# An mLSTM block feeding a two-layer FFN: another order of the front, and low weight words made by ScalarE

## The chip, the cores and the metric

The kernel runs on one core of a Trainium2 chip. The metric is the device time of one execution in microseconds (us), the median of several runs. Engines are named as in the profile: PE is TensorE's matmul part and PEld its weight load, DVE is VectorE, ACT is ScalarE, POOL is GpSimd, SP is SyncE, which issues nearly all DMAs.

## The reference

An mLSTM recurrence over 4 batches, 8 heads, 768 steps and a head size of 40 gives `y`; its 3072 rows of 320 numbers go through a feed-forward network of width 2048 with a piecewise square as activation:

```python
for t in range(S):
    m_new = np.maximum(f_gate[:, :, t] + m, i_gate[:, :, t])
    f_stab = np.exp(f_gate[:, :, t] + m - m_new)
    i_stab = np.exp(i_gate[:, :, t] - m_new)
    C = f_stab * C + i_stab * np.einsum('bhd,bhe->bhde', vt, kt)
    n = f_stab * n + i_stab * kt
    y[:, :, t] = o * np.einsum('bhde,bhe->bhd', C, qt) / np.maximum(np.abs(nq), 1.0)
...
h = x @ w_in
g = np.where(h >= 1, h, np.where(h <= -1, 0.0, (h + 1) ** 2 / 4))
return g @ w_out
```

The attention inputs are float32. The two weight matrices are float64; the kernel loads their words as they are and makes float32 numbers of them itself.

## The kernel before, in words

**Units.** The sequence is cut into 6 chunks of 128 steps. A unit `n` is one chunk of one batch: `n = 4 * chunk + batch`, 24 in all. A unit gives 128 rows of `x`; four units of one chunk make a block of 512 rows, `X[j]`, in a high part `xh` and a rest `xl`.

**FFN.** For each block `j` and each of 16 slices `fc` of the width, `mm1` (line 744) makes 8 matmuls into a PSUM tile `psh` (two of them exist), ScalarE makes `Relu` and square of it and VectorE the result `r`, which also frees the `psh` tile. `mm2` (line 765) runs two slices behind (`LAG`) and adds the product of `r` and the second weights into four `pso` tiles. In block 0 the result `r` is used as it is (8 matmuls named `pso<-ow,r`); later it is split in two parts, `gh` and `gl`.

**Weight pieces.** The weights come in 16 pieces, in the order of `W_ORDER`: in 0, in 1, out 0, in 2, out 1, in 3 and so on. Here piece k is the k-th of that order. "in i" holds what slices 2i and 2i+1 need in `mm1`, "out i" the same for `mm2`. `load_w` issues the DMA of a piece (768 KB or 640 KB) into `wraw`, which has two buffers. `convert` makes float32 of it: in `words` (line 372) ScalarE makes `mg` (an `Abs`), VectorE takes the sign half by a bitwise AND, GpSimd makes the low half (`halves[:, :, 0]`), VectorE limits `mg` and joins everything with a shift and an OR (`SCALAR_TENSOR_TENSOR win<-mg,win` or `ow<-mg,ow`). For "in" pieces `split` (line 392) then makes the high part `wh` (ScalarE copy) and the rest `wl` (VectorE subtraction).

**The front.** Before the FFN starts, units 0 to 3 are worked through in an order that is written out by hand in `STEPS`. Each step's instructions stand on their engine's queue in that order (`InOrder`; such instructions have line 85 in the profile, the others line 82). The letters that matter: `E`, `A` make the exponents in PSUM and `x` their `Exp` on ScalarE (`Abc`, or `A` for unit 3); `s` the scores and `m` their product with the decays on VectorE; `u` the output matmuls, `y` the division on VectorE (from `z` to `y` in the profile), `z` the transposes and `t` the copies into `xh` and `xl`; `v` a scaling on GpSimd; `w` the number of dummy matmuls that `hot` puts ahead of the next group. `c` converts the words of piece 0, and asks for piece 2; `e` and `d` make its `wh` and `wl`. `b` is `batch_maxima`, the running maximum of the gates of chunks 1 to 4, which sends its result through four small DMAs to `m_b`; `g1` is `batch_sums` (line 199), six VectorE instructions and the store of `a_d`, from which the decays `Abc` of later units are loaded. `batch_tail` (line 211), seven VectorE instructions, and `batch_exps`, which makes the factors `G` and `nA` from transposes, run after the first `mm1`.

**What follows the front.** Loads for chunk 1 are issued; then the loop over slices begins. In block 0 each slice is preceded by `split_next` until `DUE(fc) = 3 + fc` pieces are converted, and each converted piece asks for the piece after the next. `behind(("x", "act"), ("x", "dve"))` puts these conversions on ScalarE and VectorE behind the last `xh`, `xl` copies of a unit that was traced before them. `slot` places the attention work of units 4 to 23 between the slices. The order on each engine outside the front is fixed when the program is built, by a planner with a timing of its own.

Of the kernel before, what the change touches and what calls it, by code (L numbers as in the profile page):

```python
# [23 lines left out]
P = 128  # L24
# [30 lines left out]


STEPS = (
# [3 lines left out]
)  # L61

HALF = 64
# [35 lines left out]
def mlstm_ffn_kernel(ctx, tc, qk, qn, vk, og, fi0, fi, fib, w_in, w_out, cst, out):  # L99
# [37 lines left out]
                            base=0, channel_multiplier=-1)  # L137
    half = const.tile([P, 1], F32, name="half")
    nc.vector.memset(half, 0.5)


    a_d = dr.tile([NC, NSEQ, L], F32, name="a_d")
# [109 lines left out]
    def run(steps):  # L252
        for _ in steps:
            pass
# [47 lines left out]
    def gate_tail(c):  # L302
        i, m, a, ac, al, ex = gtail.pop(c)
        dh = m[:, :L]
        eng = nc.vector
        eng.tensor_tensor(out=a, in0=i, in1=m[:, 1:], op=ALU.subtract)
        eng.tensor_tensor(out=a, in0=a, in1=al, op=ALU.subtract)
        nc.gpsimd.tensor_copy(ex[0:32], a)
        yield
        eng.tensor_tensor(out=dh, in0=ac[:, L - 1:].broadcast_to([NSEQ, L]), in1=ac, op=ALU.subtract)  # L310
        eng.tensor_tensor(out=dh, in0=dh, in1=a, op=ALU.add)
        yield
        eng.tensor_tensor(out=ex[32:64], in0=dh, in1=al[:, L - 1:].broadcast_to([NSEQ, L]), op=ALU.add)
        eng.tensor_tensor(out=dc[:, c:c + 1], in0=ac[:, L - 1:], in1=al[:, L - 1:], op=ALU.add)
# [57 lines left out]
    def words(out, raw):  # L372

        n = raw.shape[1] * raw.shape[2] // 2
        hi = raw.rearrange("p k (f w) -> p (k f) w", w=2)[:, :, 1]
        quarter = raw.rearrange("p k f -> p (k f)").bitcast(U16).rearrange("p (f w) -> p f w", w=4)
        out = out.rearrange("p k f -> p (k f)").bitcast(I32)
        halves = out.bitcast(U16).rearrange("p (f w) -> p f w", w=2)  # L380
        mg = stage.tile([P, n], F32, name="mg", bufs=1)
        nc.scalar.activation(mg, hi.bitcast(F32), AF.Abs, scale=65536.0)
        nc.vector.tensor_scalar(out=halves[:, :, 1], in0=quarter[:, :, 3], scalar1=0x8000, scalar2=None,
                                op0=ALU.bitwise_and)

        nc.gpsimd.tensor_scalar(out=halves[:, :, 0], in0=quarter[:, :, 1], scalar1=1 / 8192, scalar2=-4095.5 / 8192,
                                op0=ALU.mult, op1=ALU.add)
        nc.vector.tensor_scalar_max(mg, mg, TINY)
        nc.vector.scalar_tensor_tensor(out=out, in0=mg.bitcast(I32), scalar=3, in1=out,
                                       op0=ALU.logical_shift_left, op1=ALU.bitwise_or)  # L390

# [7 lines left out]
    def load_w(kind, i):  # L399
        if kind == "in":  # L400
            n = 2 * P
            raw = stage.tile([P, 3, 2 * n], I32, name="wraw", bufs=2)
            at = nc.sync.dma_start(raw.rearrange("p k f -> p (k f)"), w_in[i])
        else:
            raw = stage.tile([P, 2, 2 * DM], I32, name="wraw", bufs=2)
            at = nc.sync.dma_start(raw.rearrange("p k f -> p (k f)"), w_out[i])
        raws[kind, i] = raw
        return at

    def convert(kind, i):  # L410
        raw = raws.pop((kind, i))
        if kind == "in":
            sl = slice(2 * i * P, 2 * (i + 1) * P)
            w = stage.tile([P, 3, 2 * P], F32, name="win", bufs=1)
            words(w, raw)
            yield
            yield from split(wh[:, :, sl], wl[:, :, sl], w)
        else:
            of[i] = ow.tile([P, 656], F32, name="ow")[:, :2 * DM].rearrange("p (k e) -> p k e", k=2)
            words(of[i], raw)  # L420
            if 2 * i >= PLAIN_FC:
                yield
                yield from split_out(i)
# [101 lines left out]
    def load_A(n):  # L525
        if n >= NS:
            return
        c, b = divmod(n, B)
        t = T.setdefault(n, {})
        t["A"] = ld.tile([P, H, L], F32, name="Abc", bufs=3)  # L530
        src = a_d[c, b * H:(b + 1) * H]
        mark[n, "A"] = nc.sync.dma_start(t["A"], src.unsqueeze(0).broadcast_to([P, H, L]))
# [265 lines left out]

    InOrder.on = True
    mains = [None] * B  # L800

    for what in STEPS.split():
        n = int(what[1]) if what[1:2].isdigit() else 0
        hh = int(what[2:] or 0)
        if what == "Lg":
            first_gates()
        elif what == "Lf":
            load_batch()
        elif what == "Lc":
            nc.sync.dma_start(cs_t, cst[0:120, P:])  # L810
        elif what == "Li":
            nc.sync.dma_start(ident, cst[:, :P])
        elif what == "Lo":
            load_og(0)
        elif what[:2] == "Lq":
            load_qk(hh)
        elif what[:2] == "Lv":
            load_v2(hh)
        elif what[:2] == "Lw":
            mark["load"] = load_w(*W_ORDER[hh])  # L820
        elif what[0] == "s":
            score_mm(n)
        elif what[0] == "m":
            score_mul(n, hh)
        elif what[0] == "g":
            if n:
                batch_sums()
            else:
                run(gate_sums(n))
        elif what[0] == "b":  # L830
            batch_maxima()
        elif what[0] == "k":
            run(gate_tail(n))
        elif what[0] == "h":
            gate_exps(n)
        elif what[0] == "A":
            add_sums(n)
        elif what[0] == "E":
            exponents(n)
        elif what[0] == "p":  # L840
            first_sums()
        elif what[0] == "v":
            scale1(n)
        elif what[0] == "o":
            sigmoid(0)
        elif what[0] == "x":
            decay(n, hh)
        elif what[0] == "c":
            rest = convert(*W_ORDER[nw])
            next(rest)  # L850
            load_w(*W_ORDER[nw + 2])
            nw += 1
        elif what[0] in "ed":
            next(rest, None)
        elif what[0] == "w":
            heat = int(what[1:])
        elif what[0] in "uytz":
            if what[0] == "u":
                mains[n] = main(n)
            next(mains[n])  # L860
    InOrder.on = False
    with behind("load"):
        load_og(1)
        load_v(4)
        load_qk(4)
        load_qk(5)
        for n in range(4, 4 + NA):
            load_A(n)
    for i in range(FRONT - EARLY, FRONT):
        with behind(("x", "act"), ("x", "dve"), ("v", "pool")):  # L870
            slot(i)
# [7 lines left out]
    for x in range(NG + LAG):  # L879
        j, fc = divmod(x, NFC)  # L880
        if x < NG:
            if j == 0:
                while nw < min(len(W_ORDER), DUE(fc)):
                    split_next()
                if nw == len(W_ORDER) and late is None:
                    stages.close()
                    late = ctx.enter_context(tc.tile_pool(name="late", bufs=1, side="right"))
            if fc == 0:
                ops[j] = [ps_o.tile([P, 512], F32, name="pso") for _ in range(NTC)]
            if j == 1 and fc % 2 == 0 and fc < PLAIN_FC:  # L890
                with tc.issue_after(mark["r", "act"].ins), tc.issue_after(mark["r", "dve"].ins):
                    for _ in split_out(fc // 2):
                        pass
            if x == GATES_AT:
                load_gates(later, NC - 1, NC)
                steps = gate_steps(NC - 1)
            if x >= GATES_AT:
                with tc.issue_after(mark["r", "dve"].ins):
                    next(steps, None)
            r = mm1(j, fc)  # L900
            if x == 0:
                with tc.issue_after(mark["r", "dve"].ins):
                    batch_tail()
                    batch_exps()
            with behind(("v", "pool")):
                slot(FRONT + x)
            gs[x] = parts(r) if j or fc >= PLAIN_FC else (r,)
        if x >= LAG:
            j, fc = divmod(x - LAG, NFC)
            mm2(ops[j], fc, *gs.pop(x - LAG))  # L910
            if fc == NFC - 1:
                store(j, ops.pop(j))
# [58 lines left out]
```

## Time and profile before

| | us |
|---|---|
| median of 3 runs | 518.64 (517.13 to 519.9) |
| the profiled execution | 517.97 |
| its span, first to last instruction | 516.2 |
| mean granted TensorE clock | 0.979 |

The span is shown in three parts by the way the work lies: the front up to about 33.5 us, block 0 of the FFN with the conversions and units 4 to 7 up to about 143 us, and the other five blocks. "Idle before" in a row is the time in which the engine had nothing to do before that instruction, with the work that ended it. A row of the timeline gives start, duration, engine, line, operation, output and inputs.

### The profile page before, as it was taken

Reading aid. Unit: us, or ns where it says so; the run is one execution under the profiler, and the core shown is the slowest. Engines: PE = TensorE matmul, PEld = TensorE weight load, DVE = VectorE, ACT = ScalarE, POOL = GpSimd, SP = SyncE. Lnnn points to the kernel's source line nnn. Section 1 sums busy time; section 2 is a strip of 40 time slices with the busy share of each in tenths; the row PEclk is TensorE's granted clock in tenths of the full one; section 3 lists DMA queues with packets and bytes.
Section 4 is the critical chain, followed back from the end, with each engine's and each line's share of the span. In section 5 each row is a group of like instructions: output and inputs, shape, how many; then the busy total and the mean of one; then the engine's idle time right before and its main releaser. Section 6 shows DMA issues by size and latency. Waiting matters only on the chain.

```text
span 516.2 us, 8817 instructions
## 1 busy us (share of the span) xinstructions
PE 490.7 (95%) x3396; PEld 419.4 (81%) x3399; DVE 343.0 (66%) x621; ACT 289.1 (56%) x560; POOL 135.9 (26%) x136
## 2 busy tenths in 40 slices
PE   8985999889898999999999998999999999999996
PEld 3763877778677989988889988889888889988986
DVE  4789896679758776759696657756756745444332
ACT  4525884436087555676645567555377554455553
POOL 2324531343433333323142314403230210000000
PEclk8987999979999999999999999999999999999999
DMA  8868664364441303323223423113522000010001
GB/s 227 257 183 307 161 189 138 115 193 150 131 146 40 107 27 96 118 66 111 65 78 83 133 80 118 68 53 96 170 81 77 16 1 1 0 52 1 1 2 51
DMA packets 29646, 51.48 MB, mean 100 GB/s; under 512 B 10060, under 2 KB 19940, under 8 KB 29604
## 3 DMA queue, kind: packets, MB, share of 16 engines
q1 hardware_dynamic: 29604, 50.92, 32.4%
q8 instruction: 27, 0.44, 0.4%
q14 instruction: 15, 0.12, 0.1%
HBM read 46.80 MB, written 4.04 MB: 98 GB/s over the span
## 4 chain that ended last, share of the span: by engine, by line
PE 85%; DVE 6%; ACT 5%; DMA 3%; issue 1%; SPq 0%; ACTq 0%; DVEq 0%
PE pso L82 33%; PE psh L82 33%; PE psa L82 15%; ACT Abc L82 1%; PE pso L85 1%; DMA raw<-in_qk 1%; ACT L82 1%; PE psa L85 1%; DVE ow L82 1%; DMA wraw<-in_w_in 1%; PE psh L85 1%; ACT r L82 1%; DVE win L82 1%; DMA out<-r 1%; ACT sig L82 0%
## 5 line engine op out<-in xcount | busy, mean ns | idle before, releaser
L82 ACT ACTIVATE r<-psh,half 128x512 f32<-128x512 f32 x96 | 65.4, 685 | 111.7 <-PE psh L82 111.4
L82 DVE SCALAR_TENSOR_TENSOR r<-psh,r 128x512 f32<-128x512 f32 x96 | 65.8, 686 | 71.5 <-ACT r L82 71.3
L82 PE MATMUL psh<-xh,wh 128*128 128x512 f32 x288 | 104.3, 418 | 6.7 <-DVE r L82 6.1
L82 PE MATMUL pso<-oh,gh 128*128 128x320 f32 x320 | 100.6, 317 | 2.4 <-ACT gh L82 2.1
L82 PE MATMUL psh<-xh,wl 128*128 128x512 f32 x288 | 99.8, 401 | 0.0
L82 PE MATMUL pso<-ow,gh 128*128 128x320 f32 x320 | 99.2, 312 | 0.0
L82 PE MATMUL pso<-oh,gl 128*128 128x320 f32 x320 | 94.0, 311 | 1.6 <-DVE gl L82 1.6
L82 DVE TENSOR_TENSOR gl<-r,gh 128x512 fp32r<-128x512 f32 x80 | 62.2, 779 | 40.5 <-ACT gh L82 40.4
L82 ACT CAST gh<-r 128x512 fp32r<-128x512 f32 x80 | 49.4, 618 | 51.0 <-DVE r L82 50.4
L82 PEld LDWEIGHTS pso<-oh,gh 128*128 128x128 f32 x320 | 60.1, 188 | 7.4 <-ACT gh L82 2.5
L82 PEld LDWEIGHTS psh<-xh,wl 128*128 128x128 f32 x288 | 55.2, 192 | 13.1 <-DVE wl L85 0.4
L82 PEld LDWEIGHTS psh<-xh,wh 128*128 128x128 f32 x288 | 51.8, 194 | 15.2 <-DVE r L82 6.8
L82 PEld LDWEIGHTS pso<-ow,gh 128*128 128x128 f32 x320 | 60.2, 188 | 2.8
L82 PE MATMUL psh<-xl,wh 128*128 128x512 f32 x192 | 62.3, 405 | 0.0
L82 ACT ACTIVATE r<-r 128x512 f32<-128x512 f32 x96 | 60.4, 632 | 2.5
L82 PEld LDWEIGHTS pso<-oh,gl 128*128 128x128 f32 x320 | 58.9, 188 | 2.1 <-DVE gl L82 1.9
L82 ACT ACTIVATE Abc<-Abc,nA 128x128 f32<-128x128 f32 x160 | 49.9, 391 | 0.2
L82 POOL TENSOR_TENSOR v<-vk,G 128x328 f32<-128x328 f32 x36 | 30.6, 856 | 58.3 <-issue 45.9
L82 PEld LDWEIGHTS psh<-xl,wh 128*128 128x128 f32 x192 | 36.8, 192 | 8.6
L82 PE MATMUL pso<-ow,r 128*128 128x320 f32 x128 | 38.5, 443 | 0.5 <-DVE ow L82 0.5
L82 POOL TENSOR_SCALAR_AFFINE_SELECT Abc<-Abc 128x1024 f32<-128x1024 f32 x20 | 25.4, 1275 | 48.3 <-DMA Abc<-a_d 46.1
L82 POOL TENSOR_TENSOR m<-m 128x1024 bf16<-128x1024 f32 x12 | 24.4, 2037 | 46.4 <-DVE m L82 46.4
(203 smaller groups left out, 681.0 us busy)
## 6 DMA issues: line engine op xcount, KB each, us to landing
Abc<-a_d SPq DMA_DIRECT2D x20, 512.0 KB
raw<-in_qk SPq DMA_DIRECT2D x48, 160.0 KB
vk<-in_vk SPq DMA_DIRECT2D x20, 324.0 KB
wraw<-in_w_in SPq DMA_DIRECT2D x8, 768.0 KB
wraw<-in_w_out SPq DMA_DIRECT2D x8, 640.0 KB
sig<-in_og SPq DMA_DIRECT2D x6, 640.0 KB
out<-r SPq DMA_DIRECT2D x24, 160.0 KB
qn<-in_qn SPq DMA_DIRECT2D x20, 180.0 KB
```

What stands on the lines that cost most here:

```text
L82: r = getattr(self.engine, name)(*args, **kwargs)
L85: r = getattr(self.engine, name)(*args, **kwargs)
```

## The change

The low half of each weight piece is made by ScalarE (`Identity` with a scale and a bias tile `less`) instead of GpSimd. `words` becomes a generator that stops after the ScalarE part and, in the front, once more before the join. The order of the front is new: piece 0 (`c0`, five steps) and piece 1 (`c1`, five steps) are both converted in it, `b` comes earlier, `y`, `z`, `t` steps of units 0 to 2 stand elsewhere, and `batch_tail` becomes a front step, `k1`, behind `g1`. Piece 2 is asked for in the first `c` step, piece 3 after the loads for chunk 1.

```diff
 STEPS = (
     "Lg Li Lo Lq0 Lv0 Lq1 Lw0 Lf Lq2 Lv2 Lq3 Lw1 Lc o w9 E0 g0 p A0 k0 x00 w2 s0 x01 m00 w1 E1 A1 h0 v0 x10 m01 w2 s1 "
-    "x11 v1 m10 c w2 u0 m11 b w2 E2 A2 x20 w2 s2 y0 x21 v2 m20 m21 w2 u1 z0 w2 E3 A3 x30 e w2 s3 v3 y1 x31 t0 m30 m31 "
-    "w2 u2 z1 y2 w2 u3 t1 z2 y3 w2 t2 z3 t3 d g1 "
+    "Lg Li Lo Lq0 Lv0 Lq1 Lw0 Lf Lq2 Lv2 Lq3 Lw1 Lc o w9 E0 g0 p A0 k0 x00 w2 s0 x01 m00 w1 E1 A1 h0 v0 x10 m01 b w2 s1 "
+    "x11 v1 m10 w2 u0 m11 c0 w2 E2 A2 x20 y0 w2 s2 x21 v2 c0 c0 w2 u1 m20 m21 z0 w2 E3 A3 t0 x30 c0 y1 w2 s3 v3 x31 c1 z1 "
+    "c0 m30 m31 t1 w2 u2 c1 y2 c1 z2 w2 u3 t2 c1 y3 w2 z3 t3 c1 g1 k1 "
 )
...
+    less = const.tile([P, 1], F32, name="less")
+    nc.vector.memset(less, -4095.5 / 8192)
...
         nc.scalar.activation(mg, hi.bitcast(F32), AF.Abs, scale=65536.0)
+        nc.scalar.activation(halves[:, :, 0], quarter[:, :, 1], AF.Identity, bias=less, scale=1 / 8192)
+        yield
         nc.vector.tensor_scalar(out=halves[:, :, 1], in0=quarter[:, :, 3], scalar1=0x8000, scalar2=None,
                                 op0=ALU.bitwise_and)
-        nc.gpsimd.tensor_scalar(out=halves[:, :, 0], in0=quarter[:, :, 1], scalar1=1 / 8192, scalar2=-4095.5 / 8192,
-                                op0=ALU.mult, op1=ALU.add)
         nc.vector.tensor_scalar_max(mg, mg, TINY)
+        if front:
+            yield
...
-            words(w, raw)
+            yield from words(w, raw)
...
-            words(of[i], raw)
+            yield from words(of[i], raw)
...
         elif what[0] == "k":
-            run(gate_tail(n))
+            if n:
+                batch_tail()
+            else:
+                run(gate_tail(n))
...
         elif what[0] == "c":
-            rest = convert(*W_ORDER[nw])
-            next(rest)
-            load_w(*W_ORDER[nw + 2])
-            nw += 1
-        elif what[0] in "ed":
-            next(rest, None)
+            if n not in pieces:
+                pieces[n] = convert(*W_ORDER[n])
+            next(pieces[n], None)
+            if not nw:
+                load_w(*W_ORDER[2])
+                nw = 2
...
             load_A(n)
+        load_w(*W_ORDER[3])
...
                 with tc.issue_after(mark["r", "dve"].ins):
-                    batch_tail()
                     batch_exps()
```

More of the change, by code (lines that the diff above doesn't have):

```diff
@@ L800, in mlstm_ffn_kernel @@
     mains = [None] * B
+    pieces = {}
     for what in STEPS.split():
```

1 row of the table STEPS is left out of this document.

## The prediction, made before the changed kernel ran

> **What bounds the kernel now.** I read the page first: its chain of work that ended last says whose time the span is made of.
>
> ```profile
> PE 85%; DVE 6%; ACT 5%; DMA 3%; issue 1%; SPq 0%; ACTq 0%; DVEq 0%
> ```
>
> TensorE holds 85% of the chain, so a time is only to be had where it stands still or runs slowly. The windows show where that is among the stages that the change touches (the columns: window, its length, then busy time of PE, PEld, DVE, ACT and POOL, the granted clock, DMA share and GB/s).
>
> ```profile
> 39.00:45.20 6.20, 0.08 (x1) 0.00 (x0) 5.99 (x11) 4.45 (x7) 1.50 (x2) 0.88 0.73 262
> 45.20:52.00 6.80, 6.80 (x17) 5.03 (x18) 6.34 (x13) 3.15 (x6) 4.85 (x4) 0.61 1.01 354
> 52.00:64.00 12.00, 12.00 (x62) 9.66 (x61) 9.87 (x13) 9.99 (x26) 6.60 (x6) 1.00 0.68 160
> 64.00:76.00 12.00, 12.00 (x63) 8.97 (x61) 11.47 (x16) 10.44 (x19) 3.41 (x3) 1.00 0.69 205
> 97.00:112.00 15.00, 11.86 (x73) 9.76 (x72) 12.40 (x23) 6.04 (x13) 5.67 (x6) 0.77 0.65 206
> ```
>
> Two holes are to be seen: 39 to 45.2, where TensorE does nothing and VectorE is busy for 5.99 of 6.20 us, and 97 to 112, with 3.14 us idle. Both are followed or accompanied by a low clock (0.61 and 0.77). Between them TensorE has no idle time at all. The timeline of PE shows the first hole from both sides:
>
> ```profile
> 33.56 2.07 PE L82 MATMUL psh<-xh,wh 128*128 128x512 f32 x4 [0.57 <-ACT xh L85]
> ...
> 38.68 0.40 PE L82 MATMUL psh<-xh,wl 128*128 128x512 f32 x1
> 45.20 1.22 PE L82 MATMUL psh<-xh,wh 128*128 128x512 f32 x2 [6.12 <-DVE r L82]
> ```
>
> Slices 0 and 1 of `mm1` run from 33.56 to 39.08 (5.52 us); slice 2 needs a `psh` tile, and so the first `r` of VectorE. The chain of waits gives that `r` and the price of the cold clock after it:
>
> ```profile
> 44.46 0.70 DVE r L82
> ...
> 45.20 3.78 PE psh L82 x8
> 48.98 2.98 PE pso L82 x8
> 51.96 1.86 PE psh L82 x8
> ...
> 58.90 2.15 PE pso L82 x8
> ```
>
> The same eight matmuls take 3.78 us, then 1.86; the eight of `mm2` 2.98, then 2.15. The slow clock costs (3.78 - 1.86) + (2.98 - 2.15) = 2.75 us on top of the 6.12.
>
> What VectorE does before that `r` is in its timeline:
>
> ```profile
> 26.46 0.42 DVE L85 TENSOR_TENSOR xl<-psa,xh 128x256 fp32r<-128x256 f32 x1 [2.50 <-ACT xh L85]
> ...
> 34.30 0.96 DVE L85 TENSOR_TENSOR wl<-win,wh 128x768 fp32r<-128x768 f32 x1
> 35.18 0.28 DVE L85 TENSOR_TENSOR fi_b<-fi_b,m_b 128x128 f32<-128x128 f32 x1
> 35.38 0.53 DVE L82 TENSOR_SCALAR ow<-wraw 128x640 uint16<-128x640 uint16 x1
> ...
> 39.79 0.21 DVE L85 TENSOR_SCALAR ah_b<-fi_b 128x128 f32<-128x128 f32 x1
> 40.04 0.23 DVE L85 TENSOR_SCALAR ah_b<-ah_b 128x128 f32<-128x128 f32 x1
> 40.30 0.42 DVE L85 TENSOR_TENSOR_SCAN ac_b<-rst,ah_b 128x128 f32<-128x128 f32 x1
> ```
>
> The front's last copies end at 34.3. From there to 44.46, 10.2 us, VectorE works off `wl` of piece 0, `batch_sums`, pieces 2 and 1, and the first words of piece 3.
>
> **The change part by part.** *Piece 1 into the front.* Its three word instructions on VectorE and the `wl` of piece 0 are what the front gains; the views of the tiles `win` and `mg` give the durations (minimum, median, maximum in ns):
>
> ```profile
> L82 DVE TENSOR_SCALAR win<-wraw x7: 596/974/1470, 37.2 to 117.1; 128x768 uint16<-128x768 uint16 x7
> ```
>
> ```profile
> L82 DVE TENSOR_SCALAR mg<-mg x15: 441/490/1425, 35.8 to 133.4; 128x640 f32<-128x640 f32 x8, 128x768 f32<-128x768 f32 x7
> L82 DVE SCALAR_TENSOR_TENSOR ow<-mg,ow x8: 804/1266/1661, 42.8 to 134.3; 128x640 int32<-128x640 int32 x8
> L82 DVE SCALAR_TENSOR_TENSOR win<-mg,win x7: 942/1305/1577, 38.4 to 119.0; 128x768 int32<-128x768 int32 x7
> ```
>
> Ahead of the first `mm1` stand, newly, the AND (0.60), the limit (0.49) and the join (0.94) of piece 1 and the `wl` of piece 0 (0.96): 3.0 us. I take minima, since the low words leave GpSimd, and the long values lie where it works on the same piece. The idle 2.50 us before 26.46 could hide most of it, so 0 is the lower bound. Against that, the `Abs` and low words of piece 1 stand on ScalarE ahead of `t1`, and `z2` ahead of `u3` on TensorE, with `y2` behind two conversion steps; the upper bound is 4.5. I take 3.0: the first `mm1` starts at 36.6 and the copies of `t3` end at 37.3. Piece 0's own words only move; `b` fills the time before the second scores. `b` also sends its four small DMAs before piece 2's load and no longer behind it on SP's queue; I count nothing for that but that `batch_sums` won't wait for `m_b`. Piece 3 is asked for behind the loads of chunk 1 on that queue, among them one that waits until `sig` is free; I cost it at nothing, since its conversion isn't ahead of the first `r` any more.
>
> *From `t3` to the first `r`.* In VectorE's queue now stand `wl` of piece 1 (0.96), `g1` (two subtractions of 0.28, 0.21, 0.23, the scan with 0.42, and one more instruction of this shape at 0.28: 1.7), `k1` (one scan, 0.42, and six of at most 0.28: 2.1) and, since it is traced ahead of `mm1`, the words of piece 2 (0.53 + 0.44 + 0.80 = 1.8): 6.5 us, in place of 10.2. The first `r` runs from 43.8 to 44.5, and slice 2 starts at 44.5 in place of 45.20: **-0.7**. If the planner puts `r` ahead of piece 2 and the front grows by nothing, slice 2 starts at 45.20 - 0.7 - 1.8 - 3.0 = 39.7: -5.5. If the front grows by 4.5, +0.8. Slices 0 and 1 end at 36.6 + 5.5 = 42.1, so the hole is 2.4 us and not 6.12. Whether the clock holds over it is read from the second hole, where a wait of 1.77 was enough:
>
> ```profile
> 106.01 2.07 PE L82 MATMUL psa<-raw 40*128 40x128 f32 x14 [1.77 <-DVE hv L82]
> ```
>
> ```profile
> 108.08 5.69 PE psh L82 x16
> ```
>
> Sixteen matmuls took 5.69 us there, at 1.86 for eight they take 3.72. So the clock stays low after 2.4 us and I count **0** for it, with -2.75 as the other end. The Trainium skill (TensorE: Matmul & The Clock Gate, section "Why this matters for your kernels") would have the clock drop only after gaps of more than about 3 us; by that rule the shrunken hole would keep the clock and the sum would be 2.75 us lower. The row at 108.08, slow after 1.77 us, speaks against it, and I go by the row.
>
> *Low words on ScalarE, and what follows later.* `batch_tail` ends at 37.3 + 0.96 + 1.7 + 2.1 = 42.1, so the factors `G` and `nA` come earlier; ScalarE and GpSimd show what they hold up:
>
> ```profile
> 55.11 0.93 ACT L82 ACTIVATE mg<-wraw 128x768 f32<-128x768 f32 x1
> ...
> 56.92 4.79 ACT L82 ACTIVATE Abc<-Abc,nA 128x128 f32<-128x128 f32 x16
> ...
> 70.95 0.79 ACT L82 ACTIVATE mg<-wraw 128x640 f32<-128x640 f32 x1
> ```
>
> ```profile
> 48.06 3.94 POOL L82 TENSOR_SCALAR_AFFINE_SELECT Abc<-Abc 128x1024 f32<-128x1024 f32 x3 [1.66 <-DMA Abc<-a_d]
> ```
>
> The decays of units 4 and 5 ran at 56.92, though the first selected `Abc` was there at about 49.4. With the factors early they run at 49.4, 7.5 us sooner. At the second hole this matters: piece 11, which slice 12 needs, stands behind unit 4's last copies.
>
> ```profile
> 100.22 0.48 ACT L82 CAST xh<-psa 128x384 fp32r<-128x384 f32 x1
> ```
>
> ```profile
> 106.44 0.96 DVE L82 TENSOR_TENSOR wl<-win,wh 128x768 fp32r<-128x768 f32 x1
> ```
>
> From the copy at 100.22 to the end of `wl`, 107.40, are 7.2 us; a low word on ScalarE adds 0.9 to this, as it lies behind the `Abs` and not beside it. If the copy comes 7.5 us sooner, `wl` ends at about 100.8, and attention work fills most of the time from 97. The hole is worth 3.14 of idle time and 5.69 - 3.72 = 1.97 of clock, 5.1 in all; I take two thirds, **-3.4** (bounds 0 and -5.1).
>
> The low words themselves have no row on ScalarE. The nearest is `mg`, which reads the same words: 0.93 and 0.79. In the two windows from 52 to 76 ScalarE has 9.99 + 10.44 = 20.4 of 24.0 us; the four `mg` from 55.11 to 70.95 get four companions, 2 x 0.93 + 2 x 0.79 = 3.4, and 23.9 of 24 would be full. The earlier decays take about 3 of it away, into 45.2 to 52, where ScalarE has 6.80 - 3.15 = 3.65 idle. Cover is left, but thin: **+0.5**, bounds 0 and +5.4 (below). GpSimd loses sixteen instructions and gets nothing; what stands behind them in its queue (selections, scalings) can only come sooner, and no idle time of TensorE names GpSimd, so 0. That VectorE is disturbed less by GpSimd is worth nothing of its own while TensorE has no idle time.
>
> **The sum**: -0.7 + 0 - 3.4 + 0.5 = -3.6. The profiled execution took 517.97 us (span 516.2 and 1.8 around it), so 514.4; the median, 518.64, lies 0.7 above it. Forecast 514.4. A measurement of this kernel can tell about 0.5%, 2.6 us, from no change: faster is below 516.0, slower above 521.2.
>
> **The rivals.**
>
> - *Everything opens up (0.13).* `r` goes ahead of piece 2, the front grows by half (1.5), the clock holds and the second hole closes: -0.7 - 1.8 - 1.5 - 2.75 - 5.1 = -11.9, 506.1. For it: both holes come from VectorE's backlog. Against it: the 1.77 us row.
> - *The clock alone (0.09).* All as in the forecast, but the hole of 2.4 us is too short to lower the clock: 514.4 - 2.75 = 511.6. For it: the clock was low after 6.12 us at the first place, and at the second the 1.77 us came on top of other short waits (3.14 in all). Against it: the hole at the second place was no single long one and the clock fell all the same.
> - *The gain stays in the front (0.24).* The longer front eats the shorter queue, and the second hole stays since piece 11 still stands behind unit 4, whose place in the slices is unchanged: -0.7 + 0.9 + 0.5, 518.7. This is also the case in which the change does not do what it says: the planner may order the queues behind the front as before.
> - *ScalarE becomes the bound (0.16).* If the decays do not leave 52 to 76, ScalarE is full there and `r` comes late; it decides from the point at which the work in this stretch reaches its 24.0 us; then each of the four companions shows on TensorE: 3.4, and one wait long enough for the clock adds the 1.97 of the sixteen slow matmuls. Without the second hole's gain that is +5.4 - 0.7: 522.7. For it: 23.9 of 24. Against it: the free 3.65 us before 52. The Trainium skill (ScalarE: Activation LUTs, section "Rules for kernel authors") speaks for this rival: it puts additions and multiplications by constants on VectorE and not on ScalarE. No row of this case has such a step on ScalarE.
>
> **How the numbers follow.** The forecast, with its own range of 511 to 517, has 0.38; it gives 0.33 to faster and 0.05 to within 0.5%. The first and the second rival are faster (0.13 and 0.09), the third within (0.22, and 0.02 slower), the fourth slower (0.13, and 0.03 within). Faster 0.55, same 0.30, slower 0.15. The range leaves out the far half of the first rival and of the fourth, and the far ends of the single terms: 506 to 522.
>
> **What would show it.** A first `mm1` at 36 to 37 and its slice 2 before 45, with an idle time of 1 to 3 us ahead of it; `g1`, `k1` and piece 2 ahead of the first `r` on VectorE; `Abc` of unit 4 at about 49; PE idle by less than 1.5 us in the 15 us around slice 12. Wrong it would be if PE waits for ScalarE's `r` between 50 and 75, if the front ends after 38, or if the second hole is as wide as before.

## The result, and the profile after

The changed kernel takes 523.93 us (median of 4 runs, 523.76 to 528.05), the kernel before 519.27 in the same comparison: a ratio of 1.0126, with a 95% interval of 1.0091 to 1.0161. It is slower by 1.3%, where 514.4 had been forecast and "slower" had a chance of 0.15; the time lies above the range (506 to 522). The profiled execution took 523.76 us, 5.8 more than the one of before, with a span of 521.9 and a granted clock of 0.968. One execution of e8 (523.88 us, the profiled one) and one of e12 (534.64) ran at a low clock and took more than 1.5% longer than the fastest of their kernel; the medians, ratios and stages below leave them out.

The chain of work that ended last has the same shares as before within 2 points, so the loss is again to be looked for where TensorE stands still or runs slowly:

```profile
PE 83%; DVE 6%; ACT 6%; DMA 3%; issue 1%; SPq 1%; ACTq 0%; DVEq 0%
```

The windows of the changed kernel (window, length, busy time of PE, PEld, DVE, ACT, POOL, clock, DMA share, GB/s):

```profile
43.90:49.07 5.17, 2.27 (x9) 1.51 (x7) 4.31 (x11) 3.77 (x6) 1.57 (x2) 0.83 0.69 214
49.07:56.00 6.93, 6.93 (x16) 5.05 (x17) 6.00 (x12) 4.90 (x8) 3.41 (x3) 0.56 1.01 370
64.00:76.00 12.00, 12.00 (x61) 8.82 (x60) 6.55 (x11) 11.97 (x27) 0.00 (x0) 1.00 0.47 128
97.00:113.00 16.00, 13.41 (x81) 10.90 (x78) 11.12 (x21) 9.44 (x18) 2.28 (x3) 0.90 0.44 140
```

And the last of these windows in the kernel before:

```profile
97.00:113.00 16.00, 12.86 (x77) 10.59 (x76) 12.40 (x23) 6.62 (x14) 6.40 (x7) 0.79 0.61 197
```

Three things are to be seen. The hole ahead of slice 2 is shorter, and the clock behind it low all the same (0.56). The second hole is as it was, 2.59 us idle of 16 and 3.14 before. And ScalarE is busy for 11.97 of 12 us between 64 and 76, while TensorE is busy for all 12: TensorE does not wait for it.

The front is read from TensorE's timeline. First the kernel before, then the changed one; the first row of each is the start of `u0`, the front's first output product.

```profile
14.69 1.88 PE L85 MATMUL psh<-ow,Abc 128*128 128x41 f32 x16
28.06 1.95 PE L85 MATMUL psa<-ow,A 128*128 128x41 f32 x16
```

```profile
13.71 1.88 PE L85 MATMUL psh<-ow,Abc 128*128 128x41 f32 x16
25.74 0.52 PE L85 MATMUL pso<-ident,y 128*128 128x128 f32 x3 [1.62 <-DVE y L85]
31.65 0.88 PE L85 MATMUL psa<-ident,y 128*128 128x128 f32 x3 [2.91 <-DVE y L85]
33.17 3.48 PE L85 MATMUL psa<-ow,A 128*128 128x41 f32 x16
38.39 0.90 PE L85 MATMUL psh<-ident,y 128*128 128x128 f32 x3 [0.90 <-DVE y L85]
39.87 1.22 PE L82 MATMUL psh<-xh,wh 128*128 128x512 f32 x2 [0.57 <-ACT xh L85]
49.07 1.22 PE L82 MATMUL psh<-xh,wh 128*128 128x512 f32 x2 [2.90 <-DVE r L82]
52.65 3.59 PE L82 MATMUL pso<-ow,r 128*128 128x320 f32 x8
```

The same program run twice puts `u0` at 13.71 and at 12.46 (e12 below), so stages are best measured from `u0`. The first `mm1` came 33.56 - 14.69 = 18.87 us behind it before and 39.87 - 13.71 = 26.16 after: the front grew by 7.3 us. Product `u3` (`psa<-ow,A`) came 6.1 us later and took 3.48 us in place of 1.95. Ahead of it stands the transpose `z2`, which waits 2.91 us for `y2`. VectorE's timeline shows why `y2` is late:

```profile
15.22 1.27 DVE L85 TENSOR_TENSOR_SCAN m_r<-fi_r,m_r 32x512 f32<-32x512 f32 x1 [3.00 <-DMA fi_r<-in_fi]
...
28.78 0.60 DVE L85 TENSOR_SCALAR win<-wraw 128x768 uint16<-128x768 uint16 x1
29.27 0.55 DVE L85 TENSOR_SCALAR mg<-mg 128x768 f32<-128x768 f32 x1
...
31.01 0.49 DVE L85 TENSOR_TENSOR y<-pso,sz 128x320 f32<-128x320 f32 x1
31.42 0.95 DVE L85 SCALAR_TENSOR_TENSOR win<-mg,win 128x768 int32<-128x768 int32 x1
...
40.30 0.29 DVE L85 TENSOR_TENSOR xh<-psh,xh 64x128 fp32r<-64x128 f32 x1
...
47.12 0.53 DVE L82 TENSOR_SCALAR ow<-wraw 128x640 uint16<-128x640 uint16 x1 [0.72 <-DMA wraw<-in_w_out]
...
48.32 0.69 DVE L82 SCALAR_TENSOR_TENSOR r<-psh,r 128x512 f32<-128x512 f32 x1
```

`b` stands at the head of the queue for 3.00 us until `fi_r` has landed; piece 1's AND and limit (28.78 and 29.27) stand ahead of `y2`, which ends with the row at 31.01, and its join (31.42) ahead of `y3`. At the end, the first `r` has the AND of piece 4 and a limit ahead of it, and the AND waits for its transfer.

### The profile page after: what moved, and what is told of

It reads as the page before. It is cut to its first block, busy times and chain, and to the rows that moved or that the text cites. A ratio compares the mean times of both kernels' runs of the same rounds, so it can differ in the third digit from the quotient of the medians.

```text
span 521.9 us, 8808 instructions
## 1 busy us (share of the span) xinstructions
PE 493.9 (95%) x3396; PEld 423.1 (81%) x3399; DVE 335.1 (64%) x622; ACT 304.3 (58%) x576; POOL 113.6 (22%) x120
## 4 chain that ended last, share of the span: by engine, by line
PE 83%; DVE 6%; ACT 6%; DMA 3%; issue 1%; SPq 1%; ACTq 0%; DVEq 0%
PE psh L82 33%; PE pso L82 33%; PE psa L82 15%; DMA raw<-in_qk 2%; ACT L82 1%; PE psa L85 1%; ACT r L82 1%; ACT Abc L82 1%; DMA wraw<-in_w_out 1%; PE psh L85 1%; DVE gl L82 1%; ACT sig L82 1%; PE pso L85 1%; SPq L85 0%; DVE win L82 0%
## 5 line engine op out<-in xcount | busy, mean ns | idle before, releaser
L82 PE MATMUL pso<-oh,gl 128*128 128x320 f32 x320 | 95.3, 312 | 2.8 <-DVE gl L82 2.8
L82 DVE TENSOR_TENSOR gl<-r,gh 128x512 fp32r<-128x512 f32 x80 | 63.8, 799 | 40.6 <-ACT gh L82 40.4
L82 ACT CAST gh<-r 128x512 fp32r<-128x512 f32 x80 | 49.4, 617 | 52.3 <-DVE r L82 51.5
L82 POOL TENSOR_SCALAR_AFFINE_SELECT Abc<-Abc 128x1024 f32<-128x1024 f32 x20 | 23.9, 1199 | 58.9 <-DMA Abc<-a_d 53.6
```

What stands on the lines that cost most here:

```text
L82: r = getattr(self.engine, name)(*args, **kwargs)
```

## The experiments

All in three rounds against the kernel before, which had medians of 518.22, 518.72 and 518.54 us in the three sets (e1 to e4, e5 to e8, e9 to e12). "mm1" and "slice 2" are their starts counted from the start of `u0`, read from the same rows as above; "`m` first" says whether GpSimd makes the low part of `m` ahead of a scaling `v` in unit 9 (see e11). Two kernels with the same steps in the front, e3 and e7, differ by 0.7 us in "mm1" (23.81 and 24.50), so less than that is not read as an effect.

| kernel | median, us (runs) | ratio to before, 95% interval | mm1 | slice 2 | `m` first |
|---|---|---|---|---|---|
| before | - | - | 18.87 | 30.51 | no |
| changed | 523.93 (4) | 1.0126 [1.0091, 1.0161] | 26.16 | 35.36 | yes |
| e1_low_only | 521.38 (10) | 1.0059 [1.0033, 1.0086] | 19.52 | 31.20 | yes |
| e2_order_only | 521.65 (10) | 1.0060 [1.0037, 1.0083] | 27.60 | 36.64 | yes |
| e3_u3_first | 517.92 (10) | 1.0004 [0.9985, 1.0023] | 23.81 | 32.56 | no |
| e4_piece1_out | 521.51 (6) | 1.0076 [1.0041, 1.0111] | 24.76 | 34.47 | yes |
| e5_b_back | 524.25 (4) | 1.0112 [1.0066, 1.0159] | 25.45 | 34.12 | yes |
| e6_load_first | 517.18 (10) | 0.9976 [0.9955, 0.9996] | 22.11 | 30.74 | no |
| e7_r_first | 516.47 (7) | 0.9960 [0.9929, 0.9990] | 24.50 | 31.85 | no |
| e8_load_r | 513.67 (4) | 0.9895 [0.9864, 0.9926] | - | - | no |
| e9_y_first | 512.44 (4) | 0.9890 [0.9843, 0.9937] | 18.08 | 25.36 | no |
| e10_y_gpsimd | 513.55 (4) | 0.9907 [0.9875, 0.9939] | 18.08 | 28.90 | no |
| e11_pool_order | 521.08 (10) | 1.0073 [1.0040, 1.0105] | 25.66 | 34.25 | no |
| e12_changed_again | 522.55 (3) | 1.0113 [1.0041, 1.0186] | 25.91 | 34.50 | yes |

**e1 and e2: one half of the change each.** e1 is the kernel before with the low words on ScalarE; e2 is the changed kernel with the low words on GpSimd.

```diff
+        nc.scalar.activation(halves[:, :, 0], quarter[:, :, 1], AF.Identity, bias=less, scale=1 / 8192)
-        nc.gpsimd.tensor_scalar(out=halves[:, :, 0], in0=quarter[:, :, 1], scalar1=1 / 8192, scalar2=-4095.5 / 8192,
-                                op0=ALU.mult, op1=ALU.add)
```

That is the edit of e1 on the kernel before, besides the bias tile `less`; e2 has its reverse on the changed kernel.

> The kernel before, with nothing changed but the low words, made by ScalarE. Theory 1 (the order of the front costs the time: TensorE holds the ready matmuls of unit 3 behind transposes that wait for VectorE): within 0.5% of before, 516 to 521 us, first mm1 at 33.1 to 34.2, the wait ahead of slice 2 at 5 to 7 us. Theory 2 (the low words on ScalarE cost the time, by lengthening each piece's conversion and filling ScalarE): 522 us or more, with PE waiting for ScalarE or for a later r.

> The changed kernel with the low words back on GpSimd; the new order, piece 1 in the front and the early batch tail stay. Theory 1: 521 to 526 us, first mm1 at 38.5 to 41. Theory 2: 516 to 520 us, the front's end within 1 us of before (33.6). If both parts cost, first mm1 at 36 to 38.5.

Each half alone makes the kernel slower by 0.6%; the time of e1 lies between the ranges of its two theories. The two together make about the sum, but that does not show that they add: in both halves GpSimd makes `m` first, which the changed kernel pays for only once. The low words leave the front as it was (19.52, 0.65 more); what they cost lies later, in e11 and in the last section. The order carries the loss of the front (27.60), but some 1.9 us of it are e2's own. There the join of piece 1 waits for GpSimd, so that `y3` starts at 37.72 although the matmuls of `u3` end at 35.77:

```profile
36.09 0.96 DVE L85 SCALAR_TENSOR_TENSOR win<-mg,win 128x768 int32<-128x768 int32 x1 [5.47 <-POOL win L85]
```

In the changed kernel the low words of piece 1 come from ScalarE, and this wait is absent.

**e3: `u3` ahead of `z2` on TensorE**, as before; VectorE and ScalarE keep the changed order.

```diff
-    "c0 m30 m31 t1 w2 u2 c1 y2 c1 z2 w2 u3 t2 c1 y3 w2 z3 t3 c1 g1 k1 "
+    "c0 m30 m31 t1 w2 u2 c1 y2 c1 w2 u3 z2 t2 c1 y3 w2 z3 t3 c1 g1 k1 "
```

> The changed kernel with u3 put ahead of z2 on TensorE; VectorE's and ScalarE's order in the front is the same. Theory 1: the 2.9 us wait of TensorE is filled by u3 (1.9 to 2.3 us at full clock in place of 3.5), the first mm1 starts at 36.3 to 37.7 in place of 39.9, the total is 519.5 to 522.5. Rival 3 (the front is as long as VectorE's queue with piece 1 in it, whatever TensorE's order): first mm1 at 39 to 40, total 523 to 525.

517.92, no difference to before, and 6 us less than the changed kernel; that is below the range of the first theory. `u3` itself still took 3.48 us, so the swap filled the wait but did not bring the high clock that the theory counted on. This one swap brings the first `mm1` 2.35 us nearer to `u0` and slice 2 2.8 us; besides, the planner's order for unit 9 falls back to that of before, which is worth something of its own (e11). The front is not yet that of before: the first `mm1` is 4.9 us later from `u0`, and slice 2, behind a shorter hole, 2.05 us later.

**e4: piece 1 out of the front.** The `c1` steps are left out of `STEPS`, and `split_next` converts piece 1, as before.

```diff
-    "... v3 x31 c1 z1 c0 m30 m31 t1 w2 u2 c1 y2 c1 z2 w2 u3 t2 c1 y3 w2 z3 t3 c1 g1 k1 "
+    "... v3 x31 z1 c0 m30 m31 t1 w2 u2 y2 z2 w2 u3 t2 y3 w2 z3 t3 g1 k1 "
...
-                nw = 2
+                nw = 1
...
-        load_w(*W_ORDER[3])
```

> The changed kernel without piece 1 in the front: its five steps are taken out, it is converted ahead of slice 0 as before, and piece 3 is asked for after it. Rival 3: the first mm1 starts at 34 to 35.5, as VectorE has 2.1 us less ahead of it. Theory 1: the wait of z2 for y2 stays, only about 1.1 to 2 us shorter, and the first mm1 starts at 36.5 to 38.5. The wait ahead of slice 2 grows to 5 us or more by both, so that the total stays at 520 to 525.

The front gets 1.4 us shorter, and slice 2 comes 9.7 us behind the first `mm1` in place of 9.2: most of what the front gives, slice 2 keeps. TensorE's wait ahead of it is 3.35 us and not the 5 or more that was expected. With `z2` still ahead of `u3`, taking the piece out does not bring the front back.

**e5: `b` behind `m11` again.**

```diff
-    ... v0 x10 m01 b w2 s1 x11 v1 m10 w2 u0 m11 c0 w2 ...
+    ... v0 x10 m01 w2 s1 x11 v1 m10 w2 u0 m11 b c0 w2 ...
```

> The changed kernel with one step of the front put back: `b` (the running maximum over fi_r) again behind `m11`, as before; all else stays. Theory: of the 6.3 us by which the front grew, a part comes from `b` standing at the head of VectorE's queue for 3.0 us until fi_r has landed, which pushes m10, m11, y0 and piece 0's words, so that TensorE waits 1.62 and 2.91 us for `y` and goes cold. Then the 3.00 row of the scan is gone, the first mm1 is at 37 to 38.5 in place of 39.87, and the time is 521 to 522.5. Rival, the wait is hidden because piece 0's words or z2 ahead of u3 come later anyway: first mm1 at 39.5 to 40, time 523.5 to 524.

A miss for the theory: the first `mm1` comes only 0.7 us nearer to `u0`, and the time is no better. The wait for `fi_r` is gone, but TensorE then waits 3.58 us in front of `z2`, in place of 2.91 (the scan's row in VectorE's timeline, the transpose in TensorE's):

```profile
14.55 1.27 DVE L85 TENSOR_TENSOR_SCAN m_r<-fi_r,m_r 32x512 f32<-32x512 f32 x1
```

```profile
29.90 0.87 PE L85 MATMUL psa<-ident,y 128*128 128x128 f32 x3 [3.58 <-DVE y L85]
31.42 3.48 PE L85 MATMUL psa<-ow,A 128*128 128x41 f32 x16
```

While `z2` is ahead of `u3`, an earlier VectorE is spent on waiting in front of `z2`, and `u3` runs at the low clock as before.

**e6, e7, e8: on top of e3.** e6 issues the loads of `fi_r` and `fi_b` ahead of that of piece 0; e7 puts each piece's conversion, from slice 1 on, behind the `r` of the slice before; e8 does both.

```diff
-    "Lg Li Lo Lq0 Lv0 Lq1 Lw0 Lf Lq2 ..."
+    "Lg Li Lo Lq0 Lv0 Lq1 Lf Lw0 Lq2 ..."
...
-            with behind((m, "act"), (m, "dve")):
+            with behind((m, "act"), (m, "dve")), behind(("r", "act"), ("r", "dve")):
                 for _ in convert(*W_ORDER[nw]):
```

> The kernel with u3 ahead of z2 (517.92 us, first mm1 at 36.85), and the load of fi_r and fi_b issued ahead of that of weight piece 0. Theory (`b` waits for a transfer that is queued behind piece 0): the scan waits under 1 us, the first mm1 comes at 33.5 to 35.5, the time is 515 to 516.5. Rival (the front is set by the conversion steps, which then start later because piece 0 lands about a us later): first mm1 at 36.5 to 37.5, time 517.5 to 518.5.

> The kernel with u3 ahead of z2 (517.92 us), and from slice 1 on each weight piece's conversion is issued behind the r of the slice before it. Theory: the hole ahead of slice 2 is held open because the first r stands on VectorE behind the AND and the limit of pieces 3 and 4, whose transfer has not landed; then the first r ends at about 43 in place of 44.85, slice 2 starts 1.5 to 2 us sooner (43.6 to 44.1 in place of 45.60), the time is 516 to 516.5. Rival (the hole is set by k1 and the weights, r is only late beside it): slice 2 at 45.3 to 46, time 517.5 to 518.5; and if later slices then wait for the pieces that were held back, over 518.5.

> Both edits together: fi_r loaded ahead of piece 0, and each piece's conversion behind the r of the slice before. Theory, the two gains lie in different places and add: first mm1 at 33.5 to 35.5, slice 2 some 7 us behind it, time 513.5 to 515. Rival, the second takes nothing: 515 to 516.5; both take nothing: 517.5 to 518.5.

e6 in TensorE's timeline:

```profile
28.00 1.88 PE L85 MATMUL psa<-ow,A 128*128 128x41 f32 x16
...
36.77 1.22 PE L82 MATMUL psh<-xh,wh 128*128 128x512 f32 x2 [0.57 <-ACT xh L85]
```

Now `u3` stands where it stood before, 28.00 - 14.66 = 13.3 us behind `u0` (13.37 before), and runs in 1.88: with `u3` first, the load does count, 1.7 us of front against e3. The first `mm1` itself, at 36.77, is where the rival had it, because in this execution `u0` began 1.6 us later than in e3's (14.66 and 13.04); the time, 517.18, is between the theory and its rival. In e7 slice 2 starts so:

```profile
45.25 0.73 PE L82 MATMUL psh<-xh,wh 128*128 128x512 f32 x2 [1.97 <-DVE r L82]
```

It comes 7.35 us behind the first `mm1` in place of 8.75 in e3, and 516.47 us is as the theory had it. But the place of slice 2, 45.25, is nearer the rival's, since the front of this execution was longer: from `u0` slice 2 came 0.7 us sooner than in e3 (31.85 and 32.56). Both edits together give 513.67 us, 0.7% to 1.4% below the kernel before: 4.3 less than e3, where the gains of e6 and e7 alone, 0.7 and 1.5, make 2.2. The rest of 2.0 has no row here; it is about as much as such medians vary.

**e9: `y2` and `y3` first.** In e6 the front still loses 3.2 us behind `u3`. On top of e8, the steps of piece 1 are put behind the chain of the last two units, and `y3` ahead of `t2`; the order of GpSimd in unit 9 is held as before, so that the planner's choice plays no part.

```diff
-    "... v3 x31 c1 z1 c0 m30 m31 t1 w2 u2 c1 y2 c1 w2 u3 z2 t2 c1 y3 w2 z3 t3 c1 g1 k1 "
+    "... v3 x31 z1 c0 m30 m31 t1 c1 w2 u2 y2 w2 u3 z2 y3 t2 c1 w2 z3 t3 c1 c1 g1 c1 k1 "
```

> The kernel of e8 (u3 first, fi_r loaded first, r first; 514.23 us) with weight piece 1 taken off the chain of the last two units: Abs and low words of piece 1 behind t1's copy in place of ahead of it, its AND and limit behind t2, its join and low parts behind t3, and y3 ahead of t2; GpSimd's scaling of `v` ahead of the low part of `m` in unit 9, as before. Theory (what the front still loses behind u3 is what stands on VectorE and ScalarE ahead of y2 and y3: 1.0 us for t1's copy, 1.15 of AND and limit, 0.95 of the join, 0.7 of t2): in e6 the first mm1 came 22.1 us behind the start of u0's products (18.9 in the kernel before, 26.2 in the changed one); here it comes 18.5 to 20 us behind it, and the time is 510.5 to 513. Rival (the pieces' steps are then missing at slice 2, whose hole grows by what the front loses): first mm1 at 18.5 to 20, but slice 2 10 us or more behind it in place of some 8, time 513.5 to 515.

```profile
31.41 0.73 PE L82 MATMUL psh<-xh,wh 128*128 128x512 f32 x2 [0.57 <-ACT xh L85]
38.69 0.73 PE L82 MATMUL psh<-xh,wh 128*128 128x512 f32 x2 [3.19 <-DVE r L82]
...
41.50 3.07 PE L82 MATMUL pso<-ow,r 128*128 128x320 f32 x8
...
99.37 2.07 PE L82 MATMUL psa<-raw 40*128 40x128 f32 x14 [1.73 <-DVE hv L82]
```

The first `mm1` comes 18.08 us behind `u0` (13.33), 0.8 sooner than in the kernel before, 8.1 sooner than in the changed one and a little sooner than expected; its first two matmuls run at the high clock (0.73, and 1.22 in the changed kernel and in e2 to e7). Slice 2 follows 7.28 us later, no more than in e7. 512.44 us is 1.1% below the kernel before, and the lowest median of this study.

**e10: e9 with the low words on GpSimd.** The edit is that of e2.

> e9 with the low words of all pieces made by GpSimd again, as before. Theory A (the two low-word activations of a piece, 1.17 and 1.02 us, cost nothing where ScalarE has slack, and GpSimd's own were not late either): within 1 us of e9. Theory B (low words on ScalarE hold back r and the decays in the first two blocks): 1.5 to 3 us faster than e9. Theory C (low words on GpSimd hold back its scalings of `v` and with them the front, which is what the change was to cure): 1.5 to 3 us slower.

The times are 1.1 us apart, nearer to theory A's 1 us than to theory C. The profile shows where the low words do matter: the front is the same, but VectorE's join of piece 1 waits for GpSimd, and slice 2 comes 10.82 us behind the first `mm1` in place of 7.28.

```profile
34.94 0.96 DVE L85 SCALAR_TENSOR_TENSOR win<-mg,win 128x768 int32<-128x768 int32 x1 [1.95 <-POOL win L85]
```

```profile
41.72 1.22 PE L82 MATMUL psh<-xh,wh 128*128 128x512 f32 x2 [6.72 <-DVE r L82]
```

The wait is one of order. GpSimd's timeline shows the low words of piece 2 ahead of those of piece 1, and so does that of e2 (34.02 and 35.01). In e10:

```profile
32.50 1.26 POOL L82 TENSOR_SCALAR ow<-wraw 128x640 uint16<-128x640 uint16 x1 [13.07 <-DMA ow<-in_vk]
33.84 1.06 POOL L85 TENSOR_SCALAR win<-wraw 128x768 uint16<-128x768 uint16 x1
```

ScalarE had read piece 1 at 24.39, but GpSimd stood idle for 13.07 us, until the transfer that its first instruction waited for had landed. Low words on ScalarE avoid this wait; whether GpSimd with its two instructions in the other order would do as well was not run. As far as the times go, a gain from ScalarE is not shown, since the intervals overlap.

**e11 and e12: GpSimd's order in unit 9**, and the changed kernel as it is in the same rounds. `scale2(9)` is marked, and the low part of `m` of unit 9 is issued behind it.

```diff
-        nc.gpsimd.tensor_tensor(out=v2, in0=t["v"], ...
+        mark[n, "v2"] = nc.gpsimd.tensor_tensor(out=v2, in0=t["v"], ...
...
-    def parts3(x, name, eng):
+    def parts3(x, name, eng, after=None):
...
-        eng[1].tensor_tensor(out=lo, in0=rest, in1=mid, op=ALU.subtract)
+        with behind(after):
+            eng[1].tensor_tensor(out=lo, in0=rest, in1=mid, op=ALU.subtract)
...
-                        m = parts3(M[:, h:h + 8, :], "m3", (nc.vector, nc.gpsimd))
+                        m = parts3(M[:, h:h + 8, :], "m3", (nc.vector, nc.gpsimd), (9, "v2") if n == 9 else None)
```

> The changed kernel with one pair of GpSimd's instructions in unit 9 in the order that they have in the kernel before: the scaling `v` (1.18 us) ahead of the low part of `m` (2.34 us). Theory (in the changed order `m` overlaps the second `gl` of the slice on VectorE, which then takes 1.2 us longer, and TensorE waits for it a second time): the wait of 1.16 us for `gl` behind that of 1.64 is gone, and the time is 1.0 to 1.5 us below that of e12, the changed kernel as it is. Rival (it is only beside the path): no difference, 0 to 0.4 us.

> The changed kernel as it is, on the chip of e9 to e11, to compare with them in the same rounds: 522.5 to 525 us, first mm1 25.5 to 26.5 us behind the start of u0's products, two waits for `gl` near 165 us.

The two kernels run alike up to that place (slice 2 at 46.93 and 46.96). In e11, VectorE's and TensorE's timelines have:

```profile
159.83 2.37 DVE L82 TENSOR_TENSOR gl<-r,gh 128x512 fp32r<-128x512 f32 x2
```

```profile
161.10 0.85 PE L82 MATMUL pso<-oh,gl 128*128 128x320 f32 x4 [1.65 <-DVE gl L82]
```

In e12, VectorE, GpSimd and TensorE:

```profile
159.72 3.52 DVE L82 TENSOR_TENSOR gl<-r,gh 128x512 fp32r<-128x512 f32 x2
```

```profile
160.36 2.34 POOL L82 TENSOR_TENSOR m<-m 128x1024 bf16<-128x1024 f32 x1
162.66 1.18 POOL L82 TENSOR_TENSOR v<-vk,G 128x328 f32<-128x328 f32 x1
```

```profile
160.99 0.86 PE L82 MATMUL pso<-oh,gl 128*128 128x320 f32 x4 [1.65 <-DVE gl L82]
...
163.29 0.63 PE L82 MATMUL pso<-oh,gl 128*128 128x320 f32 x1 [1.15 <-DVE gl L82]
```

With `m` on GpSimd, the pair of `gl` takes 1.15 us longer, TensorE waits a second time, and its next matmul takes 0.63 us where the same one takes 0.41 in e11. The spans differ by 520.7 - 518.3 = 2.4 us, the medians by 1.5, within what was expected but with wide ranges (518.79 to 525.98, and 522.09 to 528.87), so that the times alone show no difference. That the order of unit 9 is on the path is shown by the rows; its size, 1.2 us of wait and as much again where the clock falls, rests on the two profiles. In the changed kernel's own profile the wait was 1.16 us, and the clock held (0.41).

## Why the prediction was wrong, step by step

The loss can be followed down the two profiled executions. Slice 2 comes 3.87 us later than before (49.07 and 45.20), the first `gl` matmuls of the stretch in which unit 9 lies 4.54 later (163.50 and 158.96), and the last stores, behind the second wait there of 1.16, 5.74 later (463.00 and 457.26). So two thirds of the loss are there at slice 2, although `u0` began 1 us sooner in the changed kernel. The forecast had -0.7 at slice 2, -2.9 for the second hole and the low words together, and nothing at unit 9. Two of its signs of being wrong are there: the front ends after 38, and the second hole is nearly as wide as before.

- **The front's growth, +3.0 with bounds of 0 and 4.5: the step that failed.** It was 6.3 us by the clock of the profile and 7.3 from `u0`. The prediction added the time of the new instructions on VectorE. What counts is which chain they stand in. It named `z2` ahead of `u3`, and `y2` behind two conversion steps, and folded both into the upper bound, 1.5 above the 3.0; e3, e6 and e9 take 2.35, 1.7 and 4.0 us out, one after another (26.16, 23.81, 22.11, 18.08; e9 has the edit of e7 besides). What e9 removes held piece 1's instructions ahead of `y2` and `y3`, and `y3` behind `t2`'s copies. "`b` fills the time before the second scores" was wrong: it waited 3.00 us for a load that was queued behind piece 0's, though this counted only with `u3` first, as far as e5 and e6 show, which take the wait away by different edits. And the clock fell within the front, which no term had: `u3` 3.48 in place of 1.95.
- **From `t3` to the first `r`, 7.2 us, and slice 2 at -0.7.** From the end of `t3`'s copies (40.59) to the end of the first `r` (49.01) it was 8.4 us. The planner put words of pieces 3 and 4 between the instructions of `g1` and `k1`, and one of them waited for its transfer; with them behind `r`, 1.4 us come back (e7). The hole was forecast at 2.4 us and was 2.90, so that part was nearly right; slice 2 came 3.87 us later in the profile because of the front.
- **The clock, counted as 0: right, and partly by luck.** The clock was 0.56 behind a hole of 2.90 us; the eight `pso` matmuls took 3.59 us, and 2.31 at the high clock in e7. But behind holes of 2.84 us in e3 and 3.10 in e6 it stayed high. The Trainium skill (TensorE: Matmul & The Clock Gate, section "Why this matters for your kernels") would have it fall only after about 3 us. The trace does not agree, since the clock fell in e12 after 2.32 us, and no other fixed length fits it, since it held in e6 after 3.10. In e9, after 3.19 us, the first two matmuls took 0.73, and the clock fell within the next microsecond: it is 0.80 from 39 to 40 us and 0.50 from 40 to 41, and the eight `pso` matmuls took 3.07. The chains of e6 and e9, and e12's timeline:

```profile
45.40 2.12 PE psh L82 x8
```

```profile
38.69 3.02 PE psh L82 x8
```

```profile
46.96 1.22 PE L82 MATMUL psh<-xh,wh 128*128 128x512 f32 x2 [2.32 <-DVE r L82]
```

- **The second hole, -3.4: failed in its mechanism.** In the changed kernel `G` came at 59.47 and the decays at 61.40, not at 49.4:

```profile
61.40 4.80 ACT L82 ACTIVATE Abc<-Abc,nA 128x128 f32<-128x128 f32 x16
```

  That alone would leave the idea standing. But in e9 they did run at 49.54, and the hole was there all the same, 2.58 us idle of 16, with the same wait of 1.73 us for `hv`:

```profile
49.54 4.50 ACT L82 ACTIVATE Abc<-Abc,nA 128x128 f32<-128x128 f32 x15
```

```profile
86.00:102.00 16.00, 13.42 (x84) 10.65 (x83) 11.01 (x21) 9.62 (x18) 3.37 (x4) 0.86 0.46 139
```

  Earlier decays do not move unit 4's later steps, which are bound to slices: its last copy on ScalarE (`xh`) came 55.0 us behind slice 2 before (100.22), 55.4 in the changed kernel (104.45) and 54.9 in e9 (93.56). This was the third rival's reason, and its case for the second hole is what happened. There is more that the prediction had the other way round. It let piece 11 wait for unit 4; but what TensorE waits for is `hv`, a step of the attention, and on VectorE's queue the limit and the join of piece 11 stand ahead of the second half of `hv`. In the kernel before:

```profile
104.18 1.37 DVE L82 SCALAR_TENSOR_TENSOR win<-mg,win 128x768 int32<-128x768 int32 x1
105.47 0.49 DVE L82 TENSOR_TENSOR hv<-psa,hv 128x328 f32<-128x328 f32 x1
```

  The changed kernel and e9 have the same order there. No run moves the join, so that it holds the hole open is read from the queue and not shown.
- **The low words, +0.5, and ScalarE as the bound.** The size of one such instruction was off: `mg`'s 0.93 and 0.79 were taken, and they took more, by the views of the tiles `win` and `ow`:

```profile
L82 ACT ACTIVATE win<-wraw,less x6: 1146/1169/1179, 41.7 to 123.2; 128x768 uint16<-128x768 uint16 x6
```

```profile
L82 ACT ACTIVATE ow<-wraw,less x8: 992/1018/1031, 40.4 to 137.1; 128x640 uint16<-128x640 uint16 x8
```

  ScalarE was full from 64 to 76 as feared, and TensorE did not wait for it there, so the fourth rival did not occur, though its time, 522.7, was near the one measured. The Trainium skill (ScalarE: Activation LUTs, section "Rules for kernel authors") puts additions and multiplications on VectorE and not on ScalarE. As to the price, the trace agrees: 1.17 us against 0.60 for VectorE's AND on as many words. A loss of time from it is not shown (e9 against e10).
- **GpSimd, 0: wrong.** The planner put `m` ahead of `v` in unit 9, which costs 1.2 us of wait, and 2.4 in all where the clock falls (e11 against e12). The removed instructions are not needed for this: e2, which has them on GpSimd, shows the same order, and so does e1. Why the planner turns it is not shown. The prediction asked only whether TensorE waited for GpSimd and not whether VectorE does.

Two things stay open. One is whether the low words cost anything beside the order: e2's median is 0.9 to 2.3 us below that of the changed kernel (522.55 in e12 and 523.93), and its range overlaps that of e12 only. Its profiled execution has the same span, 521.9, but was the slowest of the ten. The other is how much of the 0.6% of e1 is the order of unit 9, whose wait is 1.14 us in its profile, and how much the clock (below).

## What to carry to other kernels

Instructions that are put into the gaps of an engine are priced by the chain behind them, not by their duration: look for the next wait of the bottleneck, and put them behind the work that ends it. In a queue that keeps its order, a step that waits must not stand ahead of one that could run, on TensorE (`z2` ahead of `u3`) as on VectorE (`b` ahead of its load, an AND ahead of its transfer) and on GpSimd (piece 2's low words ahead of piece 1's). Where a planner fixes the rest of the order, compare that order between the two kernels before a small difference is read as the price of the edit.

## What the runs showed of the hardware that was not expected

The clock does not follow from the waits alone. In e1 and in the kernel before, the same instructions come after the same two waits; in e1, then in the kernel before:

```profile
131.14 1.95 PE L82 MATMUL psa<-v,Abc 128*128 128x41 f32 x16 [0.80 <-DVE xh L82]
...
134.70 7.58 PE L82 MATMUL pso<-ow,r 128*128 128x320 f32 x16 [0.39 <-DVE ow L82]
```

```profile
131.92 1.95 PE L82 MATMUL psa<-v,Abc 128*128 128x41 f32 x16 [0.79 <-DVE xh L82]
...
135.48 4.57 PE L82 MATMUL pso<-ow,r 128*128 128x320 f32 x16 [0.49 <-DVE ow L82]
```

The sixteen matmuls take 7.58 us in the one and 4.57 in the other; what else sets the clock is not shown here. 3.0 us is as much as the whole effect of e1, whose ten runs go from 519.16 us at a mean clock of 0.980 to 524.21 at 0.965. So the time of this kernel, with its many waits of about a microsecond, spreads by 1%, and one profile is no measure of it.
